# Feed-forward work by half blocks at the head of a fused top-k attention and SwiGLU kernel

## The chip, the cores and the metric

The kernel runs on one core of one Trainium2 chip. The metric is device time in microseconds (us), the median of several executions. One execution of each kernel was also taken by the hardware profiler; times inside the kernel, counted from the start of its span, come from that trace.

## The reference

Two stages are joined. The first is attention with a top-k mask: for each of 8 batches and 8 heads, with 576 positions and 64 channels a head, a query keeps only its 32 largest scores. The second is a SwiGLU feed-forward network (FFN below) on the 8 x 576 = 4608 tokens of 512 channels that the attention gives.

```python
scores = scale * np.matmul(q, k.transpose(0, 1, 3, 2))           # (8, 8, 576, 576)
kth = np.partition(scores, -32, axis=-1)[..., -32:-31]
scores = np.where(scores >= kth, scores, -1000000000.0)
scores = scores - np.max(scores, axis=-1, keepdims=True)
attn = np.exp(scores)
attn = attn / (np.sum(attn, axis=-1, keepdims=True) + 1e-09)
attn_out = np.matmul(attn, v)
x = attn_out.transpose(0, 2, 1, 3).reshape(4608, 512)
g = x @ w_gate                                                   # (512, 1536)
silu = g * (1.0 / (1.0 + np.exp(-g)))
out = (silu * (x @ w_val)) @ w_out                               # (1536, 512)
```

Everything is float32.

## The kernel before

**Attention by units.** The attention is cut into 160 units. A unit is one batch, one slice of 128 queries and one pair of heads; the fifth slice of a batch has only 64 queries, and its two heads share the 128 partitions, so it counts as one head. A batch is therefore 20 units: sixteen with two heads, then four with one. The units are numbered 0 to 159 below. Their stages are spread over several turns of one loop (line 716). In turn n:

- VectorE (DVE) runs the top-k of unit n (`select`): for each head four MAX8 instructions (L339) with three MATCH_REPLACE8 between them (L343), then one comparison with the 32nd largest score (L349).
- GpSimd (POOL) and ScalarE (ACT) finish unit n-1: `penalize` adds the mask to the scores on POOL (L361), `weigh` takes the exponential on ACT (L370). DVE inverts a row sum (L382), and `normalize` scales unit n-2 on ACT (L385).
- TensorE (PE) transposes unit n-3 (`turn`, L397), multiplies unit n-4 by the values (`values`, L417 and L426) and makes the scores of unit n+1 (`scores`, L318, or L304 for one head). ACT copies each of these out of PSUM (L398, L441, L323 or L309). L441 writes the FFN's input `xT`.

**FFN by blocks.** The 4608 tokens are 18 blocks of 256 tokens. The generator `feed(kb)` emits one block in pieces. First come 24 pieces of gate and value products, four matmuls of 256 columns each (L480); two pieces make one product, which has one PSUM tile of three (`ps_f`). Behind a gate product ACT runs three instructions (`gate`, L505 to L507) and POOL one multiplication (L508); behind a value product ACT runs one copy and POOL one multiplication (L512, L513). Then comes the output product. In block 0 it is plain (L526, twelve pieces of two 512-column matmuls); in all later blocks it is a Strassen product in 14 pieces of three matmuls (`quarter`, L566), each counted as 0.75.

**Weights.** The weights are loaded and rounded in 36 pieces during the first units (`weights`, `rounded`). Each takes two steps on ACT (L115, L117), one on POOL (L120), one on DVE and POOL (L124, L127) and one on DVE (L130). `dve` moves this work forward by a step now and then between the top-k instructions. `need(n)` moves it forward on the spot when a product wants a weight piece that is not there.

**Order.** Every engine's instructions are chained in the order in which the program emits them (end of the function), so an engine never takes a later instruction ahead of one that waits. What decides the overlap is therefore where `pieces` is called in a turn (up to 2, then 1, 1 and 6), and how many pieces a turn gets. That number is a credit: a piece is emitted only while the credit is at least 1. In turns 0 to 27 (`HEAD`) a unit adds 4.45 (two heads) or 2.25 (one head), and up to 8 are saved up. From turn 28 on a unit adds `share(n)`, 4.4 for an ordinary two-head unit, and at most one piece is carried over. In the last turns the credit is 8. A block may begin only when all its 256 tokens are in `xT` (L659). Pieces that are left after the last unit are emitted at the end.

Of the kernel before, what the change touches and what calls it, by code (L numbers as in the profile page):

```python
# [8 lines left out]
AF = mybir.ActivationFunctionType  # L9
ALU = mybir.AluOpType  # L10
FP32 = mybir.dt.float32
# [4 lines left out]
P = 128  # L16
# [4 lines left out]
BLK = 256  # L21
# [6 lines left out]
def kernel(  # L28
# [49 lines left out]
    scale = 1.0 / float(D) ** 0.5  # L78
# [8 lines left out]
    ffn = ctx.enter_context(tc.tile_pool(name="ffn", bufs=2))  # L87
# [13 lines left out]
    wg = consts.tile([P, KC, DFF], FP32, name="wg")  # L101
    wv = consts.tile([P, KC, DFF], FP32, name="wv")
# [105 lines left out]
    T = {i: [] for i in range(1, 8)}  # L208
    weight = weights()

    def rounding(n):
        for _ in range(n):
            next(weight, None)

    def need(n):

        while ready[0] < n:
            next(weight)

    pairs = [(b, hp) for b in range(B) for hp in range(NHP)]  # L220
    raw, preps = {}, {}
# [59 lines left out]
    units = [(b, qt, hp) for b in range(B) for qt in range(J + 1) for hp in range(NHP)]  # L281
    state = {}

    def n_heads(qt):

        return 1 if qt == J else 2
# [91 lines left out]
    def normalize(n):  # L378
        st = state[n]
        tot, e, heads = st.pop("tot"), st["e"], st.pop("heads")  # L380
        nh = len(heads)
        nc.vector.reciprocal(tot[:, 0:nh], tot[:, 0:nh])  # L382
        yield
        for t, hs in enumerate(heads):
            nc.scalar.mul(e[:, hs], e[:, hs], tot[:, t : t + 1])  # L385
# [20 lines left out]
    xT, done = {}, {}  # L406
# [41 lines left out]
    def store(o, g0):  # L448

        at = g0  # L450
        while at < g0 + P:
            b, c = divmod(at, S)
            j, p0 = divmod(c, P)
            n = min(g0 + P - at, S - c, P - p0)
            r0 = b * S + (c if j == J else J * p0 + j)
            dst = out[r0 : r0 + n, :] if j == J else out[r0 : r0 + J * (n - 1) + 1 : J, :]
            nc.sync.dma_start(dst, o[at - g0 : at - g0 + n, :])
            at += n

    on_act, on_pool = [], []  # L460

    def flush(queue):
        while queue:
            queue.pop(0)()

    def feed(kb):

        x = xT.pop(kb)
        hs = []

        def product(w, s, then):
            ps = ps_f.tile([P, 2, BLK], FP32, tag="f", name="f")
            need(4 * s + (2 if w is wg else 4))
            for i in range(2):
                m = 2 * s + i
                for kc in range(KC):
                    nc.tensor.matmul(  # L480
                        ps[:, i, :],
                        w[:, kc, m * P : (m + 1) * P],
                        x[:, kc, :],
                        start=(kc == 0),
                        stop=(kc == KC - 1),
                    )
                if i == 1:
                    on_act.append(lambda: then(ps))
                yield 1

        plain = kb == 0
        first, late = slice(0, P), slice(P, BLK)
# [2 lines left out]
            "p (m t) -> p m t", t=P  # L495
        )

        for s in range(MS):
            h = ffn.tile([P, 2, BLK], FP32, tag="h", name="h", bufs=MS + 1)
            hs.append(h)  # L500


            def gate(ps, h=h):
                half = ffn.tile([P, 2, BLK], FP32, tag="gv", name="half_g", bufs=3)
                nc.scalar.activation(h[:], ps[:], AF.Tanh, scale=0.5)  # L505
                nc.scalar.mul(half[:], ps[:], 0.5)
                nc.scalar.add(h[:], h[:], 1.0)  # L507
                on_pool.append(lambda: nc.gpsimd.tensor_mul(h[:], h[:], half[:]))  # L508

            def value(ps, h=h, s=s):  # L510
                val = ffn.tile([P, 2, BLK], FP32, tag="gv", name="val", bufs=3)
                nc.scalar.copy(val[:], ps[:])  # L512
                on_pool.append(lambda: nc.gpsimd.tensor_mul(h[:], h[:], val[:]))  # L513

            yield from product(wg, s, gate)
            yield from product(wv, s, value)
        o = ffn.tile([P, 2, DM], FP32, tag="o", name="o", bufs=1)
        if plain:
            for t in range(2):
                ps = ps_f.tile([P, DM], FP32, tag="f", name="o_ps")  # L520
                for m in range(MC):
                    need(4 * MS + m + 1)
                    if m == 6:
                        flush(on_act)
                        flush(on_pool)
                    nc.tensor.matmul(  # L526
                        ps[:],
                        hs[m // 2][:, m % 2, t * P : (t + 1) * P],
                        wo[:, m, :],
                        start=(m == 0),  # L530
                        stop=(m == MC - 1),
                    )
                    if m == MC - 1:

# [113 lines left out]
    todo = list(range(NBLK))  # L648
    current = []

    def piece():

        if len(on_act) > 1:
            flush(on_act)
        if len(on_pool) > 1:
            flush(on_pool)
        while True:
            if not current:
                if not todo or done.get(todo[0], 0) < NHP * BLK:  # L659
                    return 0  # L660
                flush(on_act)
                flush(on_pool)
                current.append(feed(todo.pop(0)))
            cost = next(current[0], 0)
            if cost == 0:
                current.pop()
                continue
            return cost

    def fetch(n):  # L670

        b, qt, hp = units[n]
        i = b * NHP + hp
        if qt == 0:
            yield from prep(i)
        if qt == J and i + NHP < len(pairs):
            load(i + NHP)

    def share(n):


        others = 0.0
        for m, cost in ((n + 1, 0.7), (n - TURN, 0.6), (n - VALUES, 0.7)):
            others += cost * (0.5 if units[m][1] == J else 1)
        if units[n + 2][1] == 0:
            others += 0.6
        return 6.4 * n_heads(units[n][1]) / 2 - others

    def pieces(n):
        for _ in range(n):  # L690
            if credit[0] >= 1:
                credit[0] -= piece()

    def run(steps):
        for _ in steps:
# [14 lines left out]
    credit = [0.0]  # L710
    no = iter(())
    over = {}
    TURN, VALUES = 3, 4
    HEAD = 28
    due = [2.0]
    for n in range(NU + VALUES):
        nh = n_heads(units[n][1]) if n < NU else 1
        topk = select(n) if n < NU else no
        over[n - 1] = normalize(n - 1) if 0 <= n - 1 < NU else no
        nxt = scores(n + 1) if n + 1 < NU else no  # L720
        ahead = fetch(n + 2) if n + 2 < NU else no
        norm = over.pop(n - 2, no)

        def dve(k, beside=True):

            for _ in range(k * nh):
                next(topk, None)
                due[0] += 5 / 11 if beside else 0
                if due[0] >= 1:
                    due[0] -= 1  # L730
                    rounding(1)

        if n >= NU - NHP:
            credit[0] = 8.0
        elif n < HEAD:
            credit[0] = min(credit[0] + (4.45 if nh == 2 else 2.25), 8.0)
        else:
            credit[0] = min(credit[0] + share(n), share(n) + 1)
        flush(on_act)
        if 0 <= n - 1 < NU:  # L740
            penalize(n - 1)
        flush(on_pool)
        if 0 <= n - TURN < NU:
            run(turn(n - TURN))
        if n >= VALUES:
            finish_unit(n - VALUES)
        next(nxt, None)

        early[0]()
        if 0 <= n - 1 < NU:  # L750
# [24 lines left out]
    while piece():  # L775
        pass
# [48 lines left out]
```

## Time and profile before

| | before |
|---|---|
| median of 3 runs | 1839.66 us (1838.29 to 1840.6) |
| span of the profiled execution | 1838.0 us |
| PE busy | 1708.0 us, 93% |
| DVE busy | 1616.3 us, 88% |
| ACT busy | 1205.6 us, 66% |
| POOL busy | 1014.3 us, 55% |

The last top-k instruction ends at about 1740 us, and from there PE finishes the FFN. DVE's share of busy time is thus over a span of which the last 5% has no work for it. In the first 100 us there is no FFN work, and PE is far less busy than later; from 370 us on PE is busy nearly all the time. The stages have different limits, so the shares of the whole span don't say what the change is worth: it acts on the units before 31, which begin before 374 us.

### The profile page before, as it was taken

How to read it: one execution, taken by the hardware profiler on the slowest of the kernel's cores; microseconds unless marked ns; L12 is line 12 of the kernel's file. 1: busy time of each engine (PE TensorE's matmuls, PEld its weight loads, DVE VectorE, ACT ScalarE, POOL GpSimd, SP SyncE). 2: the span in 40 equal slices, each digit the busy share in tenths (PEclk: the TensorE clock that was granted, in tenths of full speed). 3: DMA queues.
4: the chain of work that ended last, by engine and by line, in shares of the span. 5: the costliest groups of instructions: out<-in, count | busy, mean ns of one | idle time of the engine just before them, and what ended most of it. 6: DMA issues, size and time to landing. Idle time of an engine off the chain costs nothing.

```text
span 1838.0 us, 30521 instructions
## 1 busy us (share of the span) xinstructions
PE 1708.0 (93%) x10756; PEld 1408.7 (77%) x10756; DVE 1616.3 (88%) x3405; ACT 1205.6 (66%) x2943; POOL 1014.3 (55%) x932
## 2 busy tenths in 40 slices
PE   3448899999999989999999999999999999999998
PEld 2336668777888878887888878888788878888887
DVE  7999999998999889997999989998999989998400
ACT  5667667677676667676767676767776766675431
POOL 3556755645555545655464646564556554646444
PEclk7668999999999999999999999999999999999999
DMA  7322121000300021000300012000300011000000
GB/s 189 101 87 86 58 66 27 12 1 19 75 1 12 1 66 27 12 1 14 73 19 1 12 40 53 1 12 2 73 19 12 1 36 32 1 12 12 1 13 12
DMA packets 109145, 59.65 MB, mean 32 GB/s; under 512 B 88512, under 2 KB 96704, under 8 KB 108992
## 3 DMA queue, kind: packets, MB, share of 16 engines
q1 hardware_dynamic: 107936, 57.44, 12.0%
q8 instruction: 85, 1.39, 0.3%
q14 instruction: 68, 0.56, 0.1%
q10 hardware_dynamic: 1056, 0.26, 0.1%
HBM read 48.23 MB, written 9.44 MB: 31 GB/s over the span
## 4 chain that ended last, share of the span: by engine, by line
PE 83%; ACT 2%; POOL 2%; DVE 1%; issue 1%; DMA 0%; POOLq 0%; ACTq 0%
PE f L480 39%; PE x_ps L566 9%; PE av L426 8%; PE etps L397 7%; PE s L318 7%; PE y_ps L566 6%; PE s L304 2%; PE av L417 1%; PE o_ps L526 1%; PE kqps L273 1%; DVE m L339 1%; POOL p L552 0%; ACT e L370 0%; DVE rest L343 0%; POOL h L614 0%
## 5 line engine op out<-in xcount | busy, mean ns | idle before, releaser
L339 DVE MAX8 m<-rest 128x8 f32<-128x576 f32 x864 | 621.6, 764 | 2.2
L343 DVE MATCH_REPLACE8 rest<-m,rest 128x576 f32<-128x576 f32 x576 | 428.7, 760 | 0.0
L361 POOL TENSOR_TENSOR e<-e,sc 128x1152 f32<-128x1152 f32 (+1 forms) x160 | 382.8, 2393 | 71.2 <-DVE e L349 66.2
L480 PE MATMUL f<-xT,wg 128*128 128x256 f32 x1728 | 401.7, 382 | 0.0
L480 PE MATMUL f<-xT,wv 128*128 128x256 f32 x1728 | 398.9, 381 | 0.0
L480 PEld LDWEIGHTS f<-xT,wg 128*128 128x128 f32 x1728 | 322.8, 190 | 62.5 <-issue 20.5
L480 PEld LDWEIGHTS f<-xT,wv 128*128 128x128 f32 x1728 | 324.5, 190 | 58.6 <-issue 16.4
L508 POOL TENSOR_TENSOR h<-h,half_g 128x512 f32<-128x512 f32 x108 | 138.6, 1283 | 299.0 <-ACT h L507 292.5
L339 DVE MAX8 m<-sc 128x8 f32<-128x576 f32 x288 | 206.9, 760 | 109.4 <-ACT sc L309 58.6
L370 ACT ACTIVATE e<-e,bias 128x576 f32<-128x576 f32 x288 | 222.7, 779 | 87.4 <-POOL e L361 87.2
L397 PE MATMUL etps<-ident,e 128*128 128x128 f32 (+1 forms) x1312 | 185.8, 287 | 99.3 <-POOL size L120 40.5
L398 ACT COPY et<-etps 128x512 f32<-128x512 f32 (+1 forms) x448 | 184.8, 485 | 123.7 <-PE etps L397 122.7
L397 PEld LDWEIGHTS etps<-ident,e 128*128 128x128 f32 (+1 forms) x1312 | 159.2, 147 | 128.4 <-POOL size L120 43.4
L513 POOL TENSOR_TENSOR h<-h,val 128x512 f32<-128x512 f32 x108 | 139.8, 1295 | 193.6 <-ACT val L512 193.5
L385 ACT ACTIVATE e<-e,tot 128x576 f32<-128x576 f32 x288 | 212.3, 791 | 4.5 <-DVE tot L382 4.5
L343 DVE MATCH_REPLACE8 rest<-m,sc 128x576 f32<-128x576 f32 x288 | 213.5, 755 | 0.0
L318 PE MATMUL s<-kqT 64*128 64x288 f32 x1024 | 172.7, 449 | 4.0 <-ACT kqT L278 3.1
L349 DVE TENSOR_SCALAR e<-sc,m 128x576 f32<-128x576 f32 x288 | 170.2, 636 | 3.4
L426 PE MATMUL av<-et,v 128*64 128x128 f32 (+1 forms) x2560 | 172.1, 280 | 0.0
L323 ACT COPY sc<-s 128x288 f32<-128x288 f32 x512 | 164.5, 404 | 2.5 <-PE s L318 2.5
L426 PEld LDWEIGHTS av<-et,v 128*64 128x64 f32 x2560 | 135.6, 144 | 22.7 <-issue 6.8
L505 ACT ACTIVATE h<-f 128x512 f32<-128x512 f32 x108 | 65.5, 606 | 132.0 <-PE f L480 132.0
(71 smaller groups left out, 2020.5 us busy)
## 6 DMA issues: line engine op xcount, KB each, us to landing
v<-in_v_dram SPq DMA_DIRECT2D x32, 256.0 KB, 3.0
kq_in<-in_k_dram SPq DMA_DIRECT2D x63, 128.0 KB, 2.8
kq_in<-in_q_dram SPq DMA_DIRECT2D x63, 128.0 KB, 3.0
w<-in_moe_w_gate_dram SPq DMA_DIRECT2D x12, 512.0 KB, 3.7
w<-in_moe_w_val_dram SPq DMA_DIRECT2D x12, 512.0 KB, 3.8
w<-in_moe_w_out_dram SPq DMA_DIRECT2D x12, 512.0 KB, 3.6
out_dram<-o SPq DMA_DIRECT2D x40, 128.0 KB, 2.4
out_dram<-o SPq DMA_DIRECT2D x16, 256.0 KB, 2.4
```

The source lines that it names most:

```text
L318: nc.tensor.matmul(ps[:, 0:half], slab[d, q0 : q0 + P], slab[d, k0 : k0 + half])
L339: nc.vector.max(m[:, t, 8 * r : 8 * r + 8], cur[:, hs])
L343: nc.vector.match_replace(rest[:, hs], m[:, t, 8 * r : 8 * r + 8], cur[:, hs], LOWEST)
L349: nc.vector.tensor_scalar(e[:, hs], sc[:, hs], m[:, t, TOP_K - 1 : TOP_K], FAR, ALU.is_lt, ALU.mult)
L361: nc.gpsimd.tensor_tensor(e[:, every], e[:, every], sc[:, every], ALU.add)
L370: nc.scalar.activation(e[:, hs], e[:, hs], AF.Exp, bias=bias[:, t : t + 1], scale=scale, accum_out=tot[:, t : t + 1],)
L385: nc.scalar.mul(e[:, hs], e[:, hs], tot[:, t : t + 1])
L397: nc.tensor.transpose(ps[0:kl, c * P : (c + 1) * P], e[:, k0 : k0 + kl], ident[:])
L398: nc.scalar.copy(et[0:kl, c0 : c0 + cn, :], ps[0:kl, 0 : cn * P].rearrange("p (c j) -> p c j", c=cn),)
L426: nc.tensor.matmul(av[hh * R : (hh + 1) * R, 0:ql], v_last[:, hh, :] if c == J else vt[:, hh, c, :], moving, start=last and c == 0, stop=c ...
L480: nc.tensor.matmul(ps[:, i, :], w[:, kc, m * P : (m + 1) * P], x[:, kc, :], start=(kc == 0), stop=(kc == KC - 1),)
L566: nc.tensor.matmul(ps, lhsT, T[i][m], start=m == 0, stop=m == MQ - 1)
```

## The change

For blocks 0 and 1 the gate and value products are made in two halves of 128 tokens. The first half may begin when half of the block's tokens are there. The yield of a piece is now its size, 0.5 for a half. The credit of the head goes: all turns use `share(n)`, in which a two-head unit is worth 7.0 instead of 6.4 until the Strassen combinations of the weights have been made, and carry at most one piece over. Where a weight piece is missing, the generator gives 0 and waits for a later turn (`until`) instead of moving the rounding forward. The purpose is to start FFN work about four units earlier, while PE has little to do, and to give each unit what its top-k leaves room for.

```diff
-    def need(n):
+    def until(n):
         while ready[0] < n:
-            next(weight)
+            yield 0
...
+    def parts(kb):
+        return [slice(0, P), slice(P, BLK)] if kb < 2 else [slice(0, BLK)]
...
-        def product(w, s, then):
+        def product(w, s, c, then):
+            n = c.stop - c.start
+            yield from until(4 * s + (2 if w is wg else 4))
             ps = ps_f.tile([P, 2, BLK], FP32, tag="f", name="f")
-            need(4 * s + (2 if w is wg else 4))
             for i in range(2):
                 m = 2 * s + i
                 for kc in range(KC):
                     nc.tensor.matmul(
-                        ps[:, i, :],
+                        ps[:, i, 0:n],
                         w[:, kc, m * P : (m + 1) * P],
-                        x[:, kc, :],
+                        x[:, kc, c],
...
-                yield 1
+                yield n / BLK
...
+        for c in parts(kb):
+            while done[kb] < NHP * c.stop:
+                yield 0
+            for s in range(MS):
...
+                yield from product(wg, s, c, gate)
+                yield from product(wv, s, c, value)
...
-                if not todo or done.get(todo[0], 0) < NHP * BLK:
+                if not todo or done.get(todo[0], 0) < NHP * parts(todo[0])[0].stop:
                     return 0
...
-        return 6.4 * n_heads(units[n][1]) / 2 - others
+        beside = 6.4 if T[1] else 7.0
+        return beside * n_heads(units[n][1]) / 2 - others

     def pieces(n):
-        for _ in range(n):
-            if credit[0] >= 1:
-                credit[0] -= piece()
+        while n > 0 and credit[0] >= 1:
+            size = piece()
+            if not size:
+                break
+            n -= size
+            credit[0] -= size
...
-        elif n < HEAD:
-            credit[0] = min(credit[0] + (4.45 if nh == 2 else 2.25), 8.0)
         else:
             credit[0] = min(credit[0] + share(n), share(n) + 1)
```

More of the change, by code (lines that the diff above doesn't have):

```diff
@@ L464, in flush @@
             queue.pop(0)()
+    def parts(kb):
+        return [slice(0, P), slice(P, BLK)] if kb < 2 else [slice(0, BLK)]
     def feed(kb):
-        x = xT.pop(kb)
+        x = xT[kb]
         hs = []
-        def product(w, s, then):
+        def product(w, s, c, then):
+            n = c.stop - c.start
+            yield from until(4 * s + (2 if w is wg else 4))
             ps = ps_f.tile([P, 2, BLK], FP32, tag="f", name="f")
-            need(4 * s + (2 if w is wg else 4))
             for i in range(2):
@@ L487, in product @@
                 if i == 1:
-                    on_act.append(lambda: then(ps))
-                yield 1
+                    on_act.append(lambda: then(ps[:, :, 0:n], c))
+                yield n / BLK
         plain = kb == 0
@@ L496, in feed, with gate, value @@
         )
[L498 to L516, printed above, removed]
+        for c in parts(kb):
+            while done[kb] < NHP * c.stop:
+                yield 0
+            for s in range(MS):
+                if c.start == 0:
+                    hs.append(ffn.tile([P, 2, BLK], FP32, tag="h", name="h", bufs=MS + 1))
+                h = hs[s]
+                def gate(ps, c, h=h):
+                    half = ffn.tile([P, 2, BLK], FP32, tag="gv", name="half_g", bufs=3)
+                    hc, gc = h[:, :, c], half[:, :, c]
+                    nc.scalar.activation(hc, ps, AF.Tanh, scale=0.5)
+                    nc.scalar.mul(gc, ps, 0.5)
+                    nc.scalar.add(hc, hc, 1.0)
+                    on_pool.append(lambda: nc.gpsimd.tensor_mul(hc, hc, gc))
+                def value(ps, c, h=h):
+                    val = ffn.tile([P, 2, BLK], FP32, tag="gv", name="val", bufs=3)
+                    hc, vc = h[:, :, c], val[:, :, c]
+                    nc.scalar.copy(vc, ps)
+                    on_pool.append(lambda: nc.gpsimd.tensor_mul(hc, hc, vc))
+                yield from product(wg, s, c, gate)
+                yield from product(wv, s, c, value)
+        del xT[kb]
         o = ffn.tile([P, 2, DM], FP32, tag="o", name="o", bufs=1)
@@ L521, in feed @@
                 for m in range(MC):
-                    need(4 * MS + m + 1)
+                    yield from until(4 * MS + m + 1)
                     if m == 6:
@@ L663, in piece @@
                 current.append(feed(todo.pop(0)))
[L664 to L668, printed above, removed]
+            size = next(current[0], None)
+            if size is not None:
+                return size
+            current.pop()
     def fetch(n):
@@ L683, in share @@
         for m, cost in ((n + 1, 0.7), (n - TURN, 0.6), (n - VALUES, 0.7)):
-            others += cost * (0.5 if units[m][1] == J else 1)
+            if m >= 0:
+                others += cost * (0.5 if units[m][1] == J else 1)
         if units[n + 2][1] == 0:
             others += 0.6
-        return 6.4 * n_heads(units[n][1]) / 2 - others
+        beside = 6.4 if T[1] else 7.0
+        return beside * n_heads(units[n][1]) / 2 - others
     def pieces(n):
-        for _ in range(n):
-            if credit[0] >= 1:
-                credit[0] -= piece()
+        while n > 0 and credit[0] >= 1:
[4 more added lines that the diff above has]
+            credit[0] -= size
     def run(steps):
@@ L713 @@
     TURN, VALUES = 3, 4
-    HEAD = 28
     due = [2.0]
```

## The prediction

> **What bounds the kernel now.** I read the page's busy times first, then the slices, then sums by stage, then the waits of DVE alone. The busy times and slices:
>
> ```profile
> PE 1708.0 (93%) x10756; PEld 1408.7 (77%) x10756; DVE 1616.3 (88%) x3405; ACT 1205.6 (66%) x2943; POOL 1014.3 (55%) x932
> ...
> PE   3448899999999989999999999999999999999998
> ...
> DVE  7999999998999889997999989998999989998400
> ```
>
> PE looks like the bound, and its low digits stand in the first slices, where the change puts work. But in the same slices DVE is full. The stage sums say it in numbers (columns: stretch, its length, busy us of PE, weight loads, DVE, ACT, POOL with instruction counts, then PE clock, DMA share, GB/s):
>
> ```profile
> 0.00:103.35 103.35, 41.69 (x219) 30.92 (x221) 90.91 (x196) 62.18 (x142) 50.77 (x52) 0.69 0.54 139
> 103.35:374.13 270.78, 227.34 (x1378) 177.05 (x1378) 262.75 (x550) 186.60 (x446) 163.13 (x141) 0.91 0.18 53
> 374.13:1732.93 1358.80, 1342.26 (x8636) 1116.58 (x8633) 1255.84 (x2649) 926.08 (x2292) 749.95 (x683) 0.99 0.09 22
> ```
>
> Units 7 to 30 run from 103.35 to 374.13 us (a unit starts at its first MAX8). There DVE is busy for 262.75 of 270.78 us; it is the bound, and only 8.0 us of it are idle. The change can win only from those 8.0 us and from instructions that take longer than usual. DVE's waits in that stretch:
>
> ```profile
> DVE m L339 <- ACT sc L323: 4.2, 4, 1.6
> DVE size L124 <- POOL size L120: 2.3, 4, 0.7
> DVE m L339 <- ACT sc L309: 0.3, 1, 0.3
> ```
>
> The rest are gaps too short to be listed. The first row is scores that come late because PE is overloaded (at the starts of units 20, 24, 26 and 29), the second is the rounding of the weights (units 8, 9, 12, 13).
>
> **What the instruction orders say.** Comparing the two programs as built: DVE's instructions are the same, one by one, from start to end. On PE I counted the pieces between the scores of one unit and the next. From unit 31 on the counts agree: each program has emitted 70.5 pieces (blocks 0 and 1) by unit 30, because block 2's tokens are complete only then. So nothing made earlier shortens the tail; the shift of unit 31 is the whole effect. The counts in size, before against after: units 7-10, 0 against 5.5, 4.5, 1, 1 (weights missing in the last two); 11-15, 8, 4, 4, 5, 4 against 5.5, 5, 4.5, 2, 6; 16-19, 3, 2, 2, 2 against 1.5, 2, 1, 1.5; 20-25, 5, 4, 5, 4, 5, 3.75 against 5, 4.5, 5, 4.5, 4.5, 4.5; 26-28, 4.5, 4.5, 0.75 against 1.5, 0, 0.
>
> **What the skill says.** "TensorE: Matmul & The Clock Gate", section "LDWEIGHTS (loading the stationary operand)", prices a weight load by its columns, 128 / 1.2 GHz = 107 ns. The trace agrees where the moving side is also 128 columns: the four transposes at 249.62 us are 0.43 us before the next group. The same page, "What's actually happening", says that PE's clock is halved after an idle window of about 3.4 us and comes back after a busy one; the trace has 9 transposes of L397 in 1.78 us at 110.9 us, against 1.12 us at 292 us. "SBUF — State Buffer", "Who interferes with whom", says that DVE in a two-port mode and POOL block one another for a whole instruction; in units 7 to 30 I find 6.9 us by which DVE instructions exceed their median, nearly all in L349 and L130 while POOL runs.
>
> **The halves, piece by piece.** On PE a product of 256 columns is 16 instructions in 3.43 us, 214 ns each. Half as wide they can't be under 107 ns, and 190 ns is the mean of one L480 weight load if loads did not overlap. Eight loads of L318 (195 ns each) take 0.79 us in all, one every 85 ns, so they do overlap; I take 110 ns, or 1.76 us for a size of 1 against 1.71, and 125 ns for the bad end. On ACT a 512-element copy takes 594 ns and a 256-element one 381 ns (L512, L624); two halves cost 168 ns more, four such instructions a pair of products, 12 pairs: 8 us. On POOL 753 against about 1290 ns: 24 times 216 ns, 5 us. ACT and POOL have 84 and 108 us free in this stretch, so as sums these are hidden. Only queue positions matter.
>
> **Units 7 to 15.** In unit 7 PE takes half products from 104.3 us, where it was idle until 110.9. Three PSUM tiles fill, and the fourth product waits for ACT, which reaches the first gate only behind the L323 copies at 109.4. So the 5.5 end at about 115.4 instead of 104.3 + 9.7 = 114.0. PE is by then warm: transposes, values and scores take 3.7 us, so the scores of unit 9 are some 1.5 us later than in before. That stalls nobody. The queues of ACT and POOL do. In unit 8:
>
> ```profile
> 118.22 2.62 POOL L361 TENSOR_TENSOR e<-e,sc 128x1152 f32<-128x1152 f32 x1
> ...
> 122.73 1.28 ACT L323 COPY sc<-s 128x288 f32<-128x288 f32 x4
> ...
> 123.89 1.47 ACT L385 ACTIVATE e<-e,tot 128x576 f32<-128x576 f32 x2
> ...
> 125.23 0.68 ACT L115 ACTIVATE size<-w 128x512 f32<-128x512 f32 x1
> ...
> 126.07 1.14 POOL L120 TENSOR_SCALAR size<-size 128x512 f32<-128x512 f32 x1 [1.34 <-ACT size L115]
> 127.25 0.43 DVE L124 TENSOR_SCALAR size<-size 128x512 int32<-128x512 int32 x1 [0.51 <-POOL size L120]
> ```
>
> DVE already waits 0.51 us at the end of a chain L361, exponential, L323, L385, L115, L120, L124; its link L385 to L120 has no slack. The change puts two POOL multiplications ahead of L361 (2 x 0.75 = 1.5 us) and a value copy with a gate between L323 and L385 (four instructions of about 0.38 = 1.5 us). Together 3.0 us, of which the 0.3 us by which L120 overlapped with DVE here comes off: DVE waits about 2.7 us more. Queued behind L124 are unit 8's last MAX8s and the comparison, so the whole loop moves. Later units bring no repetition: 9 and 10 have no gate ahead of L385, and in 11 to 13 before has a full gate there (3 x 0.61 = 1.8 us) where after has a half gate and copy (1.5 us). I add 0.3 us for unit 9 and take off 1.0 us because POOL's multiplications are shorter where they block L349 (in units 11 to 14 such excess is 5.0 us in before). Sum +2.0 us.
>
> **Units 16 to 19.** PE gets 6 instead of 9 pieces. The late scores of units 19 and 20 cost 0.3 and 1.5 us in before; what else delays there (transposes waiting for L385, the next batch's transposes) remains. One piece less in unit 18 and dearer halves give PE 1.2 us: -1.2 us.
>
> **Units 20 to 30.** Here I follow PE's lag: when it ends a turn's pieces, counted from DVE's start of the next unit. Scores reach DVE 2.0 us after PE has issued them (292 to 297 us in before), so with 3.7 us for a turn's other PE work (2.8 to 3.3 in units 20 to 23), a lag above 10.55 - 2.0 - 3.7 = 4.9 us, or 5.8 at first, makes DVE wait. After: lag 2.6 at unit 20; the turns then take 2.8+8.8+1.1 (with key transposes), 2.9+7.9+1.0, 2.9+8.8, 3.3+7.9, 3.7+7.7, 3.7+7.7 us against 10.55. The excess over the allowance comes out as waits of about 0, 0, 1.4, 1.1, 0.8 and 0.8 us: 4.1 us. The same rows of before show 0.5 + 1.6 = 2.1 us, and another 0.6 at unit 29, of which I give back half. In units 27 to 30 PE idles instead. Sum +1.7 us.
>
> **Forecast.** +2.0 - 1.2 + 1.7 = +2.5 us, 1839.7 + 2.5 = 1842.2; I say 1842. It moves work, but from one place beside a full DVE to another, and 3.7 us either way counts as the same.
>
> **Rivals.**
> - *Faster: an emptier PE ends the waits.* For it: 4.5 us of DVE's waits are late scores, and total PE work hardly grows. If three quarters of the 8.0 us go and 1 to 2 us of port blocking with them, the time is 1839.7 - 7 = 1833. Against it: units 20 to 25 get 28 pieces where they had 26.75. Chance 0.22.
> - *Slower: the queues of ACT and POOL become the wait in several units.* For it: the chain above has no slack, and unit 7's ACT load of 9.3 us grows by 3.9 to 13.2 of 13.35. If units 7, 8, 11 and 12 each lose 2.5 us instead of one, that is +7.5; if half instructions take 125 ns, 19 sizes x 16 x 15 ns = 4.6 us more PE work in units 20 to 23, which the lag passes on. Either gives about 1847, both 1851. Chance 0.35.
> - *Same, as forecast:* 0.43.
>
> The range takes in the first rival's 1833 and most of the second: 1833 to 1850.
>
> **What would show it.** Right: DVE's instruction count unchanged and its idle time in units 7 to 30 about 10 to 11 us; one long wait of L124 for L120 near 127 us; start to start of half matmuls 107 to 115 ns; unit 31 at about 376.6 us and every later distance as before. Wrong: the first unit with a wait for L124 is none, or L124 waits in four units; units 20 to 26 without late scores; or the stretch from unit 31 to the end changing by more than 1.5 us, which would mean that PE's clock or phase at unit 31 reaches further than I allow.

## The result, and the profile after

The changed kernel takes 1857.03 us (median of 6 runs, 1855.60 to 1857.98); the kernel before, run beside it, 1839.39 us (6 runs). The ratio is 1.0096 with a 95% interval of 1.0083 to 1.0109: slower by 17.6 us. The forecast was 1842 us, and the range ended at 1850. The profiled executions differ by 17.1 us, 1855.1 against 1838.0 us.

First the page of the kernel after, its busy times and the slices of PE and DVE:

```profile
PE 1715.5 (92%) x11140; PEld 1424.4 (77%) x11140; DVE 1617.3 (87%) x3405; ACT 1208.3 (65%) x2991; POOL 1019.4 (55%) x956
...
PE   3477789889999999999999999999999999999998
...
DVE  7999979999999979998999989998998989998400
```

DVE has the same 3405 instructions and is busy 1.0 us longer. PE's work grew by 7.5 us. So none of the 17 us is work on DVE; it is idle time. PE's third slice (93 to 139 us) is indeed fuller, 7 where 4 stood, as was the purpose; but the slices behind it are emptier, 7789889 where 8899999 stood.

The stage sums of the kernel after say in which stage (columns as before; the stretches are again up to unit 7, units 7 to 30, and unit 31 up to the start of unit 159):

```profile
0.00:103.66 103.66, 40.14 (x219) 29.97 (x221) 91.95 (x195) 61.92 (x142) 50.01 (x52) 0.67 0.54 139
103.66:396.04 292.38, 239.84 (x1764) 195.97 (x1762) 264.74 (x551) 191.35 (x494) 168.66 (x165) 0.89 0.18 49
396.04:1750.03 1353.99, 1338.78 (x8634) 1114.37 (x8631) 1253.85 (x2649) 924.38 (x2292) 750.38 (x683) 1.00 0.09 22
```

The middle stretch lasts 292.38 us where it lasted 270.78: +21.6 us. DVE is busy 2.0 us longer in it (264.74 against 262.75) and idle for 292.38 - 264.74 = 27.6 us against 8.0. The last stretch is 4.8 us shorter than before, which gives back a part.

Next, DVE's waits in units 7 to 30 of the kernel after (engine, line and what it waited for; then us in total, times, longest):

```profile
DVE m L339 <- ACT sc L309: 12.3, 2, 9.1
DVE size L124 <- POOL size L120: 8.1, 4, 4.0
DVE m L339 <- ACT sc L323: 4.4, 7, 1.6
DVE wo L130 <- POOL size L127: 1.7, 1, 1.7
```

Before, L309 and L124 stood for 0.3 and 2.3 us; L323 for 4.2. Two things have grown: the waits for scores of one head, of which two are now very late, and the waits for the rounding of the weights. As shifts of the start of a unit against the kernel before, in us:

| unit | 7 | 8 | 9 | 11 | 12 | 13 | 14 | 16 | 17 | 19 | 20 | 31 | 159 |
|---|---|---|---|---|---|---|---|---|---|---|---|---|---|
| shift | 0.3 | 2.3 | 6.8 | 6.8 | 6.1 | 8.5 | 10.1 | 9.1 | 18.4 | 21.3 | 20.0 | 21.9 | 17.1 |

So there are two losses: about 9 us in units 7 to 15, and about 11 us in units 16 to 19. In units 7 to 15 DVE is busy 122.6 us against 121.2 before; 1.4 us of this loss are thus longer instructions, and the rest is waiting.

**The first loss, in units 8, 12 and 13.** From the timeline of the kernel after, in unit 8 (start and duration in us, engine, line, operation, tiles, and in brackets what the engine waited for):

```profile
125.25 1.28 ACT L323 COPY sc<-s 128x288 f32<-128x288 f32 x4
...
126.40 0.40 ACT L523 COPY val<-f 128x256 f32<-128x256 f32 x1
...
126.94 0.73 POOL L524 TENSOR_TENSOR h<-h,val 128x256 f32<-128x256 f32 x1 [2.90 <-ACT val L523]
127.74 0.73 POOL L518 TENSOR_TENSOR h<-h,half_g 128x256 f32<-128x256 f32 x1
128.55 0.61 POOL L120 TENSOR_SCALAR size<-size 128x512 f32<-128x512 f32 x1
129.20 0.43 DVE L124 TENSOR_SCALAR size<-size 128x512 int32<-128x512 int32 x1 [3.96 <-POOL size L120]
```

Read from the bottom. DVE's L124 waits 3.96 us for POOL's L120, which shows no wait of its own: it runs right behind two FFN multiplications (L524, L518; L513 and L508 in the kernel before). The first of them had stood at the head of POOL's queue for 2.90 us, because the value that it multiplies is copied out by ACT only behind the score copies. The Trainium skill, "Perfetto Trace Analysis", section "Tensor Engine Instruction (MATMUL, LD_WEIGHTS)", calls ACT, DVE and GpSimd strict FIFO; the trace agrees, with L120 held until 128.55.

In unit 12 the same steps stand in a row, again with a second multiplication (L518) between the first and the second line:

```profile
185.17 0.73 POOL L524 TENSOR_TENSOR h<-h,val 128x256 f32<-128x256 f32 x1 [2.90 <-ACT val L523]
...
186.77 0.61 POOL L120 TENSOR_SCALAR size<-size 128x512 f32<-128x512 f32 x1
187.42 0.43 DVE L124 TENSOR_SCALAR size<-size 128x512 int32<-128x512 int32 x1 [3.17 <-POOL size L120]
```

And in unit 13 DVE's L130 waits 1.70 us for POOL's L127, which runs right behind two multiplications of which the first had waited 3.43 us for ACT.

**The second loss, in units 16 and 17.** The same view, around PE's output product of block 0 (L538; L526 before):

```profile
230.27 1.13 PE L538 MATMUL o_ps<-wo,h 128*128 128x512 f32 x2 [1.74 <-DVE wo L130]
...
233.97 0.68 DVE L130 SCALAR_TENSOR_TENSOR wo<-w,size 128x512 int32<-128x512 int32 x1
...
234.71 12.37 PE L538 MATMUL o_ps<-wo,h 128*128 128x512 f32 x22 [3.31 <-DVE wo L130]
246.91 1.15 PE L397 MATMUL etps<-ident,e 128*128 128x128 f32 x9
...
249.23 1.19 PE L304 MATMUL s<-kqT 64*64 64x288 f32 x8
...
251.37 0.68 ACT L309 COPY sc<-s 128x288 f32<-128x288 f32 x2
252.15 0.76 DVE L339 MAX8 m<-sc 128x8 f32<-128x576 f32 x1 [9.14 <-ACT sc L309]
```

PE waits for DVE to round the last piece of `w_out`. Then 22 of the product's 48 instructions run in one stretch of 12.37 us, and only behind them come the transposes and the scores of unit 17. All of that output work had been emitted ahead of them. DVE so waits 9.14 us at the start of unit 17. Part of the 12.37 us is a slower PE: its granted clock was 0.50 over the first six of the 22 (234.71 to 239.98 us) and 0.99 behind them, where they start 0.43 us apart; at that rate all 22 would take about 9.5 us (an estimate from this trace). The tile view of `o_ps` sums up the idle time ahead of these instructions, PE and weight loads together:

```profile
  DVE wo L130: 32.3, 12
```

Before, this product had no such wait: it began at 216.6 us, now at 199.6. The check in `until` asks only whether the rounding has been emitted, and does not see whether DVE has done it. The program is still correct, but PE's queue can run ahead of DVE.

### The profile page after: what moved, and what is told of

It reads as the page before. It is cut to its first block, busy times and chain, and to the rows that moved or that the text cites. A ratio compares the mean times of both kernels' runs of the same rounds, so it can differ in the third digit from the quotient of the medians.

```text
span 1855.1 us, 31376 instructions
## 1 busy us (share of the span) xinstructions
PE 1715.5 (92%) x11140; PEld 1424.4 (77%) x11140; DVE 1617.3 (87%) x3405; ACT 1208.3 (65%) x2991; POOL 1019.4 (55%) x956
## 4 chain that ended last, share of the span: by engine, by line
PE 80%; DVE 4%; POOL 3%; ACT 3%; issue 2%; POOLq 0%; ACTq 0%
PE f L485 39%; PE x_ps L578 9%; PE av L426 7%; PE etps L397 7%; PE s L318 7%; PE y_ps L578 6%; PE s L304 2%; DVE m L339 2%; PE av L417 1%; DVE rest L343 1%; PE kqps L273 1%; POOL e L361 1%; PE o_ps L538 1%; ACT e L370 1%; POOL p L564 1%
## 5 line engine op out<-in xcount | busy, mean ns | idle before, releaser
L361 POOL TENSOR_TENSOR e<-e,sc 128x1152 f32<-128x1152 f32 (+1 forms) x160 | 383.1, 2395 | 75.7 <-DVE e L349 60.9
L485 PE MATMUL f<-xT,wg 128*128 128x256 f32 (+1 forms) x1920 | 408.5, 363 | 12.7 <-ACT val L523 7.2
L485 PE MATMUL f<-xT,wv 128*128 128x256 f32 (+1 forms) x1920 | 406.0, 362 | 6.7 <-DVE wv L130 6.2
L485 PEld LDWEIGHTS f<-xT,wg 128*128 128x128 f32 x1920 | 334.6, 192 | 72.0 <-issue 21.0
L485 PEld LDWEIGHTS f<-xT,wv 128*128 128x128 f32 x1920 | 335.3, 192 | 62.8 <-issue 17.4
L518 POOL TENSOR_TENSOR h<-h,half_g 128x512 f32<-128x512 f32 (+1 forms) x120 | 140.7, 1173 | 315.3 <-ACT h L517 309.7
L524 POOL TENSOR_TENSOR h<-h,val 128x512 f32<-128x512 f32 (+1 forms) x120 | 144.3, 1202 | 197.1 <-ACT val L523 196.3
L385 ACT ACTIVATE e<-e,tot 128x576 f32<-128x576 f32 x288 | 211.7, 788 | 8.7 <-DVE tot L382 8.7
L318 PE MATMUL s<-kqT 64*128 64x288 f32 x1024 | 167.5, 440 | 3.5 <-ACT kqT L278 3.2
L323 ACT COPY sc<-s 128x288 f32<-128x288 f32 x512 | 163.7, 402 | 1.7 <-PE s L318 1.7
L515 ACT ACTIVATE h<-f 128x512 f32<-128x512 f32 (+1 forms) x120 | 67.7, 564 | 136.1 <-PE f L485 136.0
```

What stands on the lines that cost most here:

```text
L318: nc.tensor.matmul(ps[:, 0:half], slab[d, q0 : q0 + P], slab[d, k0 : k0 + half])
L361: nc.gpsimd.tensor_tensor(e[:, every], e[:, every], sc[:, every], ALU.add)
L485: nc.tensor.matmul(ps[:, i, 0:n], w[:, kc, m * P : (m + 1) * P], x[:, kc, c], start=(kc == 0), stop=(kc == KC - 1),)
```

## The experiments

The kernels below are the kernel after with the edit shown. "Shift" is the start of a unit against the kernel before, from one profiled execution of each. The medians were taken over few runs in places (nomul: 1850.79 and 1854.62). All twelve:

| | median us | runs | ratio to before, 95% interval |
|---|---|---|---|
| out16 | 1855.21 | 4 | 1.0084 (1.0067 to 1.0101) |
| late | 1856.41 | 4 | 1.0089 (1.0074 to 1.0104) |
| comb | 1862.27 | 4 | 1.0119 (1.0104 to 1.0134) |
| whole | 1837.92 | 20 | 0.9990 (0.9984 to 0.9997) |
| nomul | 1852.70 | 2 | 1.0072 (1.0054 to 1.0089) |
| oneact | 1849.41 | 2 | 1.0054 (1.0036 to 1.0071) |
| even | 1850.01 | 6 | 1.0061 (1.0049 to 1.0073) |
| halves_even | 1849.41 | 4 | 1.0055 (1.0042 to 1.0068) |
| nomul2 | 1843.92 | 10 | 1.0031 (1.0022 to 1.0040) |
| whole63 | 1836.95 | 13 | 0.9991 (0.9983 to 0.9999) |
| slow_early | 1840.36 | 20 | 1.0008 (1.0002 to 1.0015) |
| both_out | 1834.75 | 11 | 0.9980 (0.9971 to 0.9989) |

**out16: block 0's output product not before turn 16.**

```diff
         if plain:
+            while at_turn[0] < 16:
+                yield 0
             for t in range(2):
```

> The changed kernel with one addition: block 0's output product may not be emitted before turn 16, when DVE has worked off the last rounding step of w_out. Theory 1 (waiting weights at the head of PE's queue): in the changed kernel PE stands in front of output matmuls whose weight rows DVE rounds only at the end of unit 15, and the transposes, values and scores behind them come late; then the 9.1 us wait before unit 17 and the 1.7 us wait of L130 in unit 13 go, and the time falls by 9 to 11 us, to about 1847. Theory 2 (too much PE work for the short units, wherever it stands): the same pieces now come in turns 16 to 28 and make DVE wait there, so the time falls by less than 4 us, to 1853 or more.

The waits before units 17 and 19 are gone: the shift falls from 9.9 us at unit 16 to 7.9 at unit 20. (The wait of L130 in unit 13, which was to go too, is still 1.2 us.) But the time is only 1.8 us better, since the shift is back at 19.8 us at unit 31. DVE's waits of this kernel from unit 20 to 30 (a line's number is one higher):

```profile
DVE m L340 <- ACT sc L324: 10.8, 5, 5.5
```

The place was right, the gain was not. The pieces taken out of turns 13 to 15 come in turns 16 to 20, and push the second block's work into turns 21 to 28, at up to 5.5 sizes a unit. The longest of the new waits, before unit 24, is one for POOL's queue, not for PE:

```profile
302.84 1.37 PE L319 MATMUL s<-kqT 64*128 64x288 f32 x8
...
308.54 0.78 ACT L371 ACTIVATE e<-e,bias 128x576 f32<-128x576 f32 x1 [5.01 <-POOL e L362]
...
311.48 0.76 DVE L340 MAX8 m<-sc 128x8 f32<-128x576 f32 x1 [5.46 <-ACT sc L324]
```

PE has finished the scores at 304.2 us. ACT copies them only at 310.4, behind an exponential that waits 5.01 us for POOL's mask (L362), and ahead of the mask POOL has run four FFN multiplications and five steps of the Strassen combinations since 295.8.

**late: in turns before 16 the first two pieces of a turn behind the normalization (L385) instead of ahead of it.**

```diff
-        pieces(2)
-        flush(on_act)
+        if n >= 16:
+            pieces(2)
+            flush(on_act)
         dve(1)
...
         flush(on_pool)
+        if n < 16:
+            pieces(2)
+            flush(on_act)
```

> The changed kernel with one move: in turns 0 to 15 the first two sizes of pieces are emitted behind the scaling of unit n-2 (L385) instead of ahead of it, so ACT's gates and POOL's multiplications stand behind the rounding step L120 that DVE waits for. Theory 1 (POOL multiplications that wait for ACT stand ahead of L120): the waits of L124 for L120, 4.0 us in unit 8 and 3.2 us in unit 12, fall below 1 us each and the time by 4 to 7 us, to about 1852. Theory 2 (PE's pieces or the ports cause the loss in these units): the waits stay within 1 us of what they were and the time within 2 us of 1857.

The wait in unit 8 falls from 4.0 to 1.2 us and that in unit 12 from 3.2 to 1.2, neither below 1 us as Theory 1 had it. Unit 11 gets a new one of 1.1 us, and in unit 13 L124 waits 2.1 where L130 waited 1.7. The shift at unit 16 is 8.0 us instead of 9.1. At each of these four places the trace has two multiplications directly ahead of the rounding step: another place in the turn moves them in front of another step, and no more.

**comb: the Strassen combinations of the weights on POOL not before turn 20.**

```diff
         lo, hi = slice(0, DM // 2), slice(DM // 2, DM)
+        while at_turn[0] < 20:
+            yield
```

> The changed kernel with one delay: POOL's combinations of w_out for the Strassen product (L181 to L197) may not be emitted before turn 20. Theory 1 (they stand ahead of POOL's L361 in the short one-head units): the 3.2 us wait before unit 19 goes, the 9.1 us wait before unit 17 stays, and the time falls by 2 to 3 us, to about 1854.5. Theory 2 (unit 19's scores are late because of PE): nothing changes by more than 1 us. Since the combinations then come beside units 20 to 23, up to 2 us may come back there.

The wait before unit 19 falls from 3.2 to 1.5 us, that before unit 17 stays at 9.0. The combinations thus have a part in the wait before unit 19 and none in that before unit 17. The time is worse, 1862.27 us. A part of that comes before unit 31 (1.4 us against the kernel after), where the credit of 7.0 lasts until the combinations are made and turns 21 to 23 get 5, 5.5 and 5 sizes. The larger part, 3.8 us, comes between units 31 and 159 (1357.8 us against 1354.0), with the same pieces in the same turns; it was not traced.

**whole: the new credit, but no halves.**

```diff
-        return [slice(0, P), slice(P, BLK)] if kb < 2 else [slice(0, BLK)]
+        return [slice(0, BLK)]
```

> The changed kernel with whole blocks everywhere: no halves, no early start, but the new credit and the new handling of missing weights. Theory 1 (the loss comes from the early start by halves): the waits of unit 8 and unit 12 are as in the kernel before and the time lies within 4 us of it, at 1840 to 1844. Theory 2 (the loss comes from the credit and from where it puts the output product): the wait before unit 17 stays at several us, and the time is 1848 or more.

1837.92 us, a little faster than before. There is no wait for L124 in units 8 and 12, and the shift at unit 31 is 1.2 us. So the credit is not the culprit; the loss is in the halves with their early start.

**nomul, oneact: less POOL or ACT work in the first halves of blocks 0 and 1.** nomul leaves out their two multiplications; oneact leaves out the scaling, the addition and the value copy on ACT as well.

```diff
-                    on_pool.append(lambda: nc.gpsimd.tensor_mul(hc, hc, gc))
+                    if c.start or kb > 1:
+                        on_pool.append(lambda: nc.gpsimd.tensor_mul(hc, hc, gc))
```

> The changed kernel without POOL's multiplications for the first halves of blocks 0 and 1 (so their gates and values are not multiplied into h; PE and ACT do all they did). It looks at units 7 to 15, where the changed kernel loses 8.8 us on the kernel before. Theory 1 (POOL: multiplications that stand ahead of the rounding in POOL's queue and block VectorE's port): unit 8's wait of 4.0 us falls to about 0.5, unit 7 loses its 2.0 us of longer VectorE instructions, and unit 11 starts less than 2.5 us later than in the kernel before, not 6.8. Theory 2 (ACT: its gates push back what the rounding and the scores need): unit 11 still starts 4 us late or more. The wait before unit 17 stays at about 9 us with both.

> As the run without multiplications, and besides ACT does only the tanh of these halves: its other two gate instructions and the value copy are left out. Theory 1 (POOL alone): no more than 1 us earlier at unit 11 than the run without multiplications. Theory 2 (ACT): the loss that the run without multiplications leaves at unit 11 goes, down to below 1.5 us. If both leave 4 us or more, the products on PE themselves delay the transposes and all behind them.

In nomul the wait of unit 8 is gone, and the shift at unit 11 is 1.8 us (6.8 in the kernel after). In oneact it is 2.4. Once the multiplications are gone, relieving ACT as well gains nothing; so ACT's load delays the rounding through the multiplications that wait for it, and not by itself. Unit 7 still loses 1.1 us in both. The waits in units 12, 13 and 17 remain in nomul (3.2, 2.2 and 9.3 us): second halves are multiplied there, and the output product is as early as before.

**even, halves_even: a flat credit of 6.0 until turn 30,** in even on top of whole, in halves_even on top of out16, late and comb.

```diff
-        beside = 6.4 if T[1] else 7.0
+        beside = 6.4 if n > 30 else 6.0
```

> Whole blocks with the new credit made smaller: 6.0 in place of 7.0 and 6.4 until turn 30, so that a two-head unit gets about 4 sizes instead of 5 and the 70 sizes last to turn 30 instead of turn 28. Theory (PE's overload in units 21 to 26 makes DVE wait, and PE idles afterwards): the waits of units 23 and 24 (2.1 us) and of unit 18 (1.5 us) fall to below 1.5 us in all, and the time is 2 to 3 us below the run with whole blocks, about 1835. Rival (those waits come from queues of ACT and POOL, not from the number of pieces): within 1 us of 1838.

> The changed kernel with four mends at once: output product of block 0 from turn 16, pieces behind L385 in turns 0 to 15, combinations of w_out from turn 20, and a credit of 6.0 until turn 30. Theory 1 (each loss has its own cause, and with the credit lowered the output product no longer returns its stall): the waits before units 17 and 19 and in units 22 to 26 go, units 7 to 15 keep about 7 us of loss, and the time is about 1845. Theory 2 (the halves give PE more to do than units 16 to 30 hold): the stalls return before unit 31, and the time is 1850 or more.

In halves_even units 20 to 30 now cost 1.0 us (6.3 us of shift at unit 20, 7.3 at 31), where they cost 11.9 in out16. It makes four edits at once and so doesn't say which of them did it; but slow_early and both_out below, which also have the output product from turn 16 and a lower credit, lose only 2.0 and 1.2 us there, and a lower credit is what the three have in common. Units 7 to 15 cost as much as ever (8.9 us at unit 16). The time is 4 us above the 1845 expected. even missed: the waits before units 24 and 25 go, but 3.8 us of waits come before units 18 and 19, and unit 31 starts at +1.6 us where it starts at +1.2 in whole. By turn 30 only 69.75 of the 70.5 sizes are out, and the pieces of 43 later turns differ from those of the kernel after. The shift grows to 12.2 us at unit 140 and is 8.4 at 159. The wait of 5.1 us before unit 37 is no sign of this: halves_even and both_out have one of 5.2 us there, with every later piece in its usual turn.

**nomul2: no POOL multiplications at all for blocks 0 and 1.**

```diff
-                    on_pool.append(lambda: nc.gpsimd.tensor_mul(hc, hc, gc))
+                    if kb > 1:
+                        on_pool.append(lambda: nc.gpsimd.tensor_mul(hc, hc, gc))
```

> The changed kernel without any of POOL's multiplications for blocks 0 and 1, both halves (gates and values are not multiplied into h there). The first run without them took away unit 8's wait but left 3.2 us in unit 12 and 2.2 us in unit 13, where the second half of block 0 is made. Theory 1 (POOL's multiplications again): both waits fall to 0.5 us or less and unit 16 starts less than 2 us later than in the kernel before, instead of 4.1. Theory 2 (PE or ACT are late in units 11 to 13): the 3.2 us of unit 12 stay. The 9 us before unit 17 stay with both: the order of the output product is not touched.

Its waits in units 7 to 30:

```profile
DVE m L339 <- ACT sc L309: 9.8, 2, 8.4
DVE m L339 <- ACT sc L323: 5.5, 5, 1.5
DVE size L124 <- POOL size L120: 0.5, 1, 0.5
```

L124 waits 0.5 us where it waited 8.1. The shift at unit 16 is -3.4 us instead of +9.1. (The kernel before has multiplications there too; taking all of them out therefore ends below zero.) The wait of 8.4 us before unit 17 stays: the two losses are independent.

**whole63: whole, with a flat credit of 6.3,** which puts all 70.5 sizes out by turn 29.

```diff
-        beside = 6.4 if T[1] else 7.0
+        beside = 6.4 if n > 30 else 6.3
```

> Whole blocks with a credit of 6.3 until turn 30 (about 4.3 sizes a two-head unit, 70.5 by turn 29, so that block 2 begins at turn 31 as in the kernel before). Theory (the run with a credit of 6.0 lost its 12 us behind unit 31, because 69.75 instead of 70.5 sizes were done by turn 30 and all later blocks stood at other places): with 70.5 in time the distance to the kernel before stays within 2 us from unit 31 on, and the waits of units 23 and 24 are smaller than with 7.0; the time is 1835 to 1838. Rival (the smaller credit itself costs, since PE then works up to unit 30 with no pause): 1843 or more.

1836.95 us, the fastest of the versions that compute everything; its interval and that of whole overlap. The shift is -3.1 us at unit 28 and +1.1 at 31, because of waits for scores before units 29 and 30; ACT stood there waiting for POOL's mask (L361). From unit 31 to 159 the shift changes by -2.3 us, where it grew by 6.8 in even, which fits the theory about the 70.5 sizes.

**slow_early: halves and early start kept, but hardly a piece in turns 7 to 10, the output product from turn 16, a credit of 6.4.**

```diff
+        if n < 11:
+            credit[0] = min(credit[0], 1.0)
         flush(on_act)
```

> Halves with an early start at a low rate: at most one half piece (0.5) in each of turns 7 to 10, output product from turn 16, credit 6.4 until turn 30. Theory 1 (the early start costs through the number of POOL multiplications in a unit): unit 8's wait of 4.0 us falls below 1 us and unit 11 starts within 2.5 us of the kernel before; unit 12 with 9 half pieces keeps 1 to 3 us; the waits before units 17 and 19 stay away; the time is 1842 to 1846. Theory 2 (halves cost in whatever number): unit 11 starts 5 us late or more and the time is 1848 or more.

1840.36 us, better than the 1842 to 1846 expected: most of the loss is gone, and nothing is won. Unit 8 doesn't wait any more, units 17 and 19 neither. But the rounding still stands behind multiplications in units 13 and 15, as the waits of its units 7 to 30 show:

```profile
DVE size L124 <- POOL size L120: 4.8, 4, 3.3
DVE wo L130 <- POOL size L127: 2.5, 1, 2.5
```

In turns 11 to 15 it makes 22 sizes of gate and value products in halves, and whole makes 24 in whole blocks, with about half as many multiplications and with no such wait. That speaks for the number of multiplications; but no run has the halves without the early start, so the two are not fully told apart.

**both_out: nomul2 and out16 together, with a credit of 6.4 until turn 30.** Halves and early start stay; the multiplications of blocks 0 and 1 are left out.

> This takes both named causes out of the kernel after at once: no POOL multiplications for blocks 0 and 1 (their products with the gate and with the value are left out), the output product of block 0 not before turn 16, and a credit of 6.4 for a two-head unit until turn 30, which still gives all 70.5 sizes by turn 29. The halves and the early start stay. Theory (the multiplications ahead of the rounding, and the output product ahead of its weights, are all that the halves cost before unit 31): the shift against the kernel before stays near -3 us at unit 16, no wait for scores of over 1 us before units 17 and 19, unit 31 between -4 and +1 us, time 1835 to 1839. Rival (half products cost by themselves too, on PE or in the queue of ACT): the shift at unit 31 is +3 us or more, time 1841 or more, with waits in other units.

1834.75 us, just below the range expected. Its eleven times lie in two groups, six from 1833.4 to 1834.8 and five from 1838.1 to 1838.7; the trace is of an execution of the second (1838.62). Its waits in units 7 to 30 (lines one higher):

```profile
DVE m L340 <- ACT sc L324: 2.3, 3, 1.4
DVE m L340 <- POOL xT L603: 1.0, 1, 1.0
DVE size L124 <- POOL size L120: 0.5, 1, 0.5
```

The shift is -2.7 us at unit 16, -4.7 at unit 20 and -3.5 at unit 31. With both causes taken out, and with the lower credit, the loss before unit 31 is gone altogether, though every half product is still made, those of block 0 nearly all in the same turns. Whatever the halves cost by themselves on PE and ACT is no more than what the missing multiplications give back. This is no version to use, since it lacks work that has to be done.

## Why the prediction was wrong, step by step

Forecast and measurement by stretch, as the change of the shift in us:

| stretch | forecast | measured |
|---|---|---|
| units 7 to 15 | +2.0 | +8.8 |
| units 16 to 19 | -1.2 | +10.9 |
| units 20 to 30 | +1.7 | +1.9 |
| from unit 31 | 0 (up to 1.5 either way) | -4.8 |

- **Right: the work.** DVE's instructions are the same 3405. In a timeline 16 half matmuls start within 1.78 us (106.42 to 108.20), 111 ns each, where 110 was estimated. POOL's half multiplications take 0.73 us. Both_out fits the view that the halves are hidden on PE and ACT, within what its missing multiplications give back.
- **Units 7 to 15: the step that failed is "Later units bring no repetition", and with it the chain.** The prediction had L124 as the place and unit 8 as the first, and priced one wait at 2.7 us through L385, L115 and L120. Measured is 3.96 us minus the 0.5 of before in unit 8 (3.5 for the 2.7), and again 3.2 us in unit 12 and 1.7 in unit 13, where none was forecast. The link was another one: the multiplications that stand directly ahead of L120 or L127 in POOL's queue and wait for ACT. The prediction counted the multiplications ahead of L361, and then asked of later units only how long ACT takes ahead of L385. nomul and nomul2 show that it was these, oneact that ACT's load does no harm without them, and late that shifting them only changes the unit. That there are twice as many of them for the same work, and so twice as many places where a rounding step can be held up, fits slow_early against whole, but is not separated from the early start.
- **The -1.0 us for shorter port blocking was right where it was placed, and left out two units.** In units 11 to 14 DVE's busy time did fall, from 56.3 to 54.6 us. In units 7 and 8, where the kernel before has no multiplications, it rose from 25.9 to 29.0, which the prediction didn't count. In unit 7 the trace shows the comparison and what runs beside it:

```profile
117.10 1.99 DVE L349 TENSOR_SCALAR e<-sc,m 128x576 f32<-128x576 f32 x2
117.33 1.44 POOL L127 TENSOR_TENSOR size<-size,w 128x512 int32<-128x512 int32 x1 [2.55 <-ACT et L398]
```

and in the kernel before:

```profile
115.85 0.97 DVE L349 TENSOR_SCALAR e<-sc,m 128x576 f32<-128x576 f32 x2
116.10 1.86 POOL L127 TENSOR_TENSOR size<-size,w 128x512 int32<-128x512 int32 x1 [2.49 <-ACT xT L441]
```

The two comparisons took 0.97 us in unit 7 before, and L127 took 1.86; now it is the comparisons that take longer. Unit 7 is 2.0 us longer without any wait on DVE, and half of that is this pair. But the halves are not its cause: in whole, which makes no FFN work before turn 11, the pair takes 1.97 us too. The Trainium skill, "SBUF — State Buffer", section "Who interferes with whom", says that a DVE instruction in a two-port mode and one of POOL block one another whole, and that the order of issue decides. The trace agrees that one of the two is drawn out; which was issued first it doesn't show, since the starts stand in the same order both times.
- **Units 16 to 19: the step that failed is the -1.2 us, from "PE gets 6 instead of 9 pieces".** It counted pieces by the turn in which they are emitted and took those of turn 15 as done in turn 15. They are output pieces, and their weights are rounded on DVE only at the end of unit 15. So PE did them in unit 16, all at once, ahead of unit 17's scores. The prediction asked for each gate and value piece whether its weight was missing, and didn't ask whether a weight that had been emitted would be ready. out16 shows it, and nomul2 that the multiplications have no part in it. Of the 3.2 us before unit 19, 1.5 are left in comb and also in nomul and nomul2, and nothing in out16. In the kernel after, ACT's exponential waits 1.6 us for POOL's mask ahead of these scores; the combinations, the multiplications and the late output product each seem to have a part; they were not told apart.
- **Units 20 to 30: the right sum, in good part by luck.** The lag of PE was followed turn by turn and came out at +1.7 us against +1.9, with 4.1 us of late scores before units 21 to 30, as measured. But it began from a state of PE that the 20 us lost before unit 20 had changed, and PE was not what most of these scores waited for. Before unit 23, the longest of these waits:

```profile
303.32 1.24 PE L318 MATMUL s<-kqT 64*128 64x288 f32 x8
...
305.23 0.78 ACT L370 ACTIVATE e<-e,bias 128x576 f32<-128x576 f32 x1 [1.58 <-POOL e L361]
...
308.17 1.42 DVE L339 MAX8 m<-sc 128x8 f32<-128x576 f32 x2 [1.58 <-ACT sc L323]
```

PE has finished the scores 2.5 us before ACT copies them (307.09); ACT had waited for POOL's mask, and the mask for a multiplication that stood 2.2 us at the head of POOL's queue. The waits before units 25 and 27 (0.4 and 1.5 us) have such a wait of ACT for POOL's mask too (0.3 and 0.6 us). In the kernel before, no wait for scores in these units has one. out16 loses 10 us more in this stretch, and the longest wait there is POOL's as well.
- **From unit 31: outside what was allowed.** Emission from turn 31 on is the same, piece by piece, in nomul2, whole63, both_out and the kernel after; measured to unit 159 this stretch costs -4.4, -2.3, +2.3 and -4.8 us. That the engines stand differently at unit 31 would be a reason, but no run shows it; and the times of one kernel, both_out, already lie 4 us apart. The gain comes in small steps at many units (44, 46, 67, 77, 93 among them). It was not traced to a mechanism and stays open.
- **Signs of being wrong.** Two came true: L124 waits in four units, though it did so before as well (0.7 us at most), and the stretch from unit 31 changed by more than 1.5 us.
- **Rivals.** "Slower: the queues of ACT and POOL become the wait in several units" had the right place for the first loss and, at 1847 us, not the second. Its sum is short: three more units at 2.5 us are 7.5 us on top of the 2.5 forecast, or about 1850. That an output product could overtake its weights was in no rival.

## What to carry to other kernels

Work that is started earlier on an idle engine can hold up what stands behind it in that queue: ask of each piece moved forward not whether its input has been emitted, but when its producer will have done it, and what stands behind it in the queue until then. Halving a piece doubles the instructions that it puts ahead of others on every engine of its chain; follow each of them to who waits behind it, above all on an engine that feeds the bound. A wait for scores is not yet a wait for PE: look when PE had finished them, and what the engine that copies them was waiting for. And an edit that removes a wait upstream has to be judged at the next stage that is full, since there the same work may come back as another wait.

## What was not expected of the hardware

POOL's L127 started 0.25 us into a pair of DVE comparisons in the kernel before and 0.23 us into it in the kernel after; the first time POOL took longer, the second time DVE, by 1.0 us, and whole, without any FFN work there, shows the second case as well. With the same pieces in the same turns from unit 31 on, the stretch to unit 159 lasted 1354.0 us in the kernel after and 1361.1 in both_out; as executions of both_out alone differ by 4 us and each kernel has one trace, the runs don't show why.
